# One FFN piece instead of two ahead of the transposes, in sixteen turns of a fused attention and FFN kernel

## The chip, the cores and the metric

The kernel runs on one core of one Trainium2 chip. A core has five engines that run beside each other, each through its own instructions in order: TensorE (PE: matmuls and transposes, results only to PSUM), VectorE (DVE), ScalarE (ACT), GpSimd (POOL) and SyncE (SP, which issues most transfers). PEld is TensorE's load of weights. The metric is the device time of one execution in microseconds.

## The reference, cut to what matters

Attention over 8 batches and 8 heads, 576 positions, 64 channels a head, that keeps only the 32 largest scores of each row, and a SwiGLU feed-forward network (FFN) behind it, all in float32:

```python
scores = scale * np.matmul(q, k.transpose(0, 1, 3, 2))          # (8, 8, 576, 576)
kth = np.partition(scores, -top_k, axis=-1)[..., -top_k:-top_k + 1]   # top_k = 32
scores = np.where(scores >= kth, scores, -1000000000.0)
attn = np.exp(scores - np.max(scores, axis=-1, keepdims=True))
attn = attn / (np.sum(attn, axis=-1, keepdims=True) + 1e-09)
attn_out = np.matmul(attn, v)
x = np.ascontiguousarray(attn_out.transpose(0, 2, 1, 3)).reshape(B * S, H * D)   # (4608, 512)
g = x @ w_gate                                                   # (512, 1536)
out = (g * (1.0 / (1.0 + np.exp(-g))) * (x @ w_val)) @ w_out     # (1536, 512)
```

## The kernel before, in words

**Units.** A unit is a batch, a tile of up to 128 query rows, and a pair of heads. A batch has five query tiles, four of 128 rows and one of 64, and four pairs of heads: 20 units, of which the first 16 are full and the last four short (their two heads share one tile of 128 partitions). There are 160 units, numbered from 0 here; 4 * NHP is 16, 9 * NHP is 36, and `units[n][1] < J` says that unit n is full.

**Turns.** The main loop runs one turn n per unit, and every turn works on several units at different stages. In program order a turn holds:
- in even turns, on TensorE, the scores of the next two units (L325, or L308 for short ones: `s`) and between them the product of the weights with v for two earlier units (L448: `av`). ScalarE scales the scores into `sc` (L330, L315) and copies `av` into the FFN's input `xT` (L465).
- `weigh(n - 1)` on ScalarE: a Prelu and an Exp that turn scores into unnormalised weights `e` (L374, L379), whose bias comes from GpSimd (L362).
- in slices, on VectorE, the search for the 32 largest of unit n: four rounds of MAX8 (L347) with a MATCH_REPLACE8 (L351) between. The first replacement of a unit writes its buffer of `e`, one of three.
- `pieces(2)`, then the pending ScalarE evictions, then `turn(n - 2)`: the transposes of the weights of unit n - 2 (L412: `etps`; nine of 128 x 128 for a full unit, five for a short one), which ScalarE copies to SBUF (L413: `et`). Then the pending GpSimd work and `pieces(1)`, `pieces(1)`.
- `normalize(n - 1)`: the reciprocal of the sums (L393, VectorE), and the multiplication of `e` by it: the first head on ScalarE (L397), the second on GpSimd (L399).
- `shift(n)` (L362), and `pieces(6)`.

In the first turns of a batch the q and k of later units are transposed as well (L271, L264: `kqps`, copied by L276, L267, L268).

**Pieces.** FFN work is cut into pieces and placed between the attention's steps. Two kinds matter. A projection piece is eight matmuls of `xT` with the gate or value weights (L517, in the first three blocks of 256 tokens; L604 later); two pieces fill one PSUM bank `f`, which ScalarE then evicts (`val` L544, or L537 to L539 for the gate) and GpSimd multiplies into `h` (L545, L540). A quarter piece is three matmuls of 128 x 256 of the output product (L670: `y_ps`, `x_ps`), which is done as seven products of halves with sums on GpSimd ahead of and behind them (L677, L685, L690, L718, L657) and evictions on ScalarE (L697, L704, L747, L759).

**Credit.** `pieces(k)` issues up to k pieces while the turn's credit is at least 1. A turn's credit is worked out beforehand (`share`); a projection piece costs 1, a quarter piece 0.75. The credit that the earlier calls leave is spent by the later ones, the last of which takes up to six pieces.

**Order.** After the loop every instruction of TensorE, VectorE, ScalarE and GpSimd is tied behind its predecessor on the same engine, so each engine runs exactly the order in which the program wrote them. Evictions and GpSimd products are kept in two lists (`on_act`, `on_pool`) and written when `flush` is called: at the start of a turn, behind the first `pieces`, behind the transposes (GpSimd's list), and in `piece` itself when more than one is pending, or when a new block begins.

**PSUM.** Of eight banks five go round among `s`, `av`, `etps` and `kqps` (pool `ps_t`) and three among `f`, `y_ps`, `x_ps` (pool `ps_f`). A tile can be written when the last reader of the tile five (three) allocations before it has finished.

Of the kernel before, what the change touches and what calls it, by code (L numbers as in the profile page):

```python
# [25 lines left out]
def kernel(  # L26
# [40 lines left out]
    J = S // P  # L67
    JP = J * P
    R = S - JP
    NHP = H // 2  # L70
# [134 lines left out]
    def rounding(n):  # L205
        for _ in range(n):
            next(weight, None)
# [73 lines left out]
    units = [(b, qt, hp) for b in range(B) for qt in range(J + 1) for hp in range(NHP)]  # L281
    state = {}

    def n_heads(qt):

        return 1 if qt == J else 2

    def scores(n):
        b, qt, hp = units[n]
        slab = preps[b * NHP + hp]  # L290
        sc = work.tile([P, 2 * S], FP32, tag="sc", name="sc", bufs=3)
        halves = [slice(0, D), slice(D, P)]
        half = S // 2

        def bank():
            return ps_t.tile([P, 512], FP32, tag="t", name="s")


        if qt == J:
            both = (slab, preps[b * NHP + hp + 1])  # L300
            banks = []
            for i in range(2):
                k0 = R + i * half
                two = [bank(), bank()]
                banks += [(i + 2 * u, ps) for u, ps in enumerate(two)]
                for u, (sl, ps) in enumerate(zip(both, two)):
                    for hh, d in enumerate(halves):
                        nc.tensor.matmul(  # L308
                            ps[halves[hh ^ u], 0:half],
                            sl[d, S + R : S + 2 * R],  # L310
                            sl[d, k0 : k0 + half],
                        )
            yield
            for i, ps in banks:
                nc.scalar.mul(sc[:, i * half : (i + 1) * half], ps[:, 0:half], scale)  # L315
            state[n + 1] = dict(sc=sc, at=S)
        else:
            q0 = S + 2 * R + qt * P
            banks = []
            for i in range(2):  # L320
                for hh, d in enumerate(halves):
                    ps = bank()
                    banks.append((i + 2 * hh, ps))
                    k0 = (1 - hh) * R + i * half
                    nc.tensor.matmul(  # L325
                        ps[:, 0:half], slab[d, q0 : q0 + P], slab[d, k0 : k0 + half]
                    )
            yield
            for i, ps in banks:
                nc.scalar.mul(sc[:, i * half : (i + 1) * half], ps[:, 0:half], scale)  # L330
        state[n] = dict(sc=sc, at=0)

    def select(n):

        nh = n_heads(units[n][1])
        sc = state[n]["sc"]
        m = small.tile([P, 2, TOP_K], FP32, tag="m", name="m")
        heads = [slice(t * S, (t + 1) * S) for t in range(nh)]
        at = state[n]["at"]
        from_ = [slice(at + t * S, at + (t + 1) * S) for t in range(nh)]  # L340
        e = work.tile([P, 2 * S], FP32, tag="e", name="e", bufs=3)
        state[n] |= dict(m=m, e=e, heads=heads, source=from_)
        cur = sc
        rounds = TOP_K // 8
        for r in range(rounds):
            for t, hs in enumerate(from_):
                nc.vector.max(m[:, t, 8 * r : 8 * r + 8], cur[:, hs])  # L347
                yield
            if r < rounds - 1:
                for t, hs in enumerate(heads):  # L350
                    nc.vector.match_replace(  # L351
                        e[:, hs], m[:, t, 8 * r : 8 * r + 8], cur[:, from_[t]], LOWEST
                    )
                    yield
                cur, from_ = e, heads
# [31 lines left out]
    def normalize(n):  # L387
        st = state[n]
        tot, e, heads = st.pop("tot"), st["e"], st.pop("heads")
        nh = len(heads)  # L390
        for t in range(nh if n >= AHEAD else 0):
            nc.vector.tensor_scalar_add(tot[:, t : t + 1], tot[:, t : t + 1], EPS)
        nc.vector.reciprocal(tot[:, 0:nh], tot[:, 0:nh])  # L393
        yield
        for t, hs in enumerate(heads):
            if t == 0 and n >= 3 * NHP:
                nc.scalar.mul(e[:, hs], e[:, hs], tot[:, t : t + 1])  # L397
            else:
                nc.gpsimd.tensor_tensor(  # L399
                    e[:, hs], e[:, hs], tot[:, t : t + 1].to_broadcast([P, S]), ALU.mult  # L400
                )
# [375 lines left out]
    def piece():  # L777

        if len(on_act) > 1:
            flush(on_act)  # L780
        if len(on_pool) > 1:
            flush(on_pool)
        for job in early_jobs[:]:
            cost = next(job, 0)
            if cost == 0:
                early_jobs.remove(job)
            elif cost is not None:
                return cost
        if early_jobs:
            return 0  # L790
        while True:
            if not current:
                if not todo or done.get(todo[0], 0) < tokens(todo[0], int(todo[0] >= HALVED)):
                    return 0
                flush(on_act)
                flush(on_pool)
                current.append(feed(todo.pop(0)))
            cost = next(current[0], 0)
            if cost == 0:
                current.pop()  # L800
                continue
            return cost or 0

    def fetch(n):

        b, qt, hp = units[n]
        i = b * NHP + hp
        if qt == 0:
            yield from prep(i)
        if qt == J and i + NHP < len(pairs):  # L810
            load(i + NHP)

    def share(n):


        others = 0.0
        for m, cost in [(m, 0.7) for m in valued(n)] + [(n - TURN, 0.6)]:
            if m >= 0:
                others += cost * (0.5 if units[m][1] == J else 1)
        others += 0.7 * len(scored(n))  # L820
        if units[n + 3][1] == 0:
            others += 0.6

        beside = 5.8 if n < AHEAD else 6.25
        least = 2.0 if n >= 3 * NHP and n % 2 == 0 else 0.0
        return max(least, beside * n_heads(units[n][1]) / 2 - others)

    def scored(n):

        ahead = [n + 1] if n < 2 else [] if n % 2 else [n + 1, n + 2]  # L830
        return [m for m in ahead if m < NU and (units[m][1] < J or m % 2 == 0)]
# [6 lines left out]
    def pieces(n):  # L838
        for _ in range(n):
            if credit[0] >= 1:  # L840
                credit[0] -= piece()
# [28 lines left out]
    for n in range(NU + 3):  # L870
        nh = n_heads(units[n][1]) if n < NU else 1
        topk = select(n) if n < NU else no
        norm = normalize(n - 1) if 0 <= n - 1 < NU else no
        nxt = [scores(m) for m in scored(n)]
        ahead = fetch(n + 3 if n else 2) if n + 3 < NU else no

        def dve(k, beside=True):

            for _ in range(k * nh):
                next(topk, None)  # L880
                due[0] += 5 / 6 if beside else 0
                if due[0] >= 1 and not (n == 0 and len(steps) == 5):
                    due[0] -= 1
                    steps.append(n)
                    rounding(1)

        if n >= NU - NHP:
            credit[0] = 8.0
        else:
            credit[0] = min(credit[0] + share(n), share(n) + 1)  # L890
        flush(on_act)
        flush(on_pool)
        if nxt and (n < 2 or len(nxt) > 1):
            run(nxt.pop(0))
        summed = finish_units(valued(n)) if valued(n) else no
        next(summed, None)
        if nxt:
            next(nxt[0])
        early[0]()
        if 0 <= n - 1 < NU:  # L900
            weigh(n - 1)
        run(summed)
        if nxt:
            run(nxt.pop())


        dve(2, beside=False)
        if n == 0:
            run(ahead)
            load(3)  # L910
            ahead = fetch(3)
        if n < NHP:
            load_v(n)
        pieces(2)
        flush(on_act)
        dve(1)
        dve(1)
        if 0 <= n - TURN < NU:
            run(turn(n - TURN))

        flush(on_pool)
        next(ahead, None)
        pieces(1)
        next(ahead, None)
        dve(1)
        pieces(1)
        if n < AHEAD:
            run(topk)
        run(norm)
        run(topk)  # L930
        if n < NU:
            shift(n)
        pieces(6)
# [50 lines left out]
```

## Time and profile before

| what | value |
|---|---|
| median of three runs | 1713.59 us (1713.14 to 1713.67) |
| the profiled execution: time, span | 1712.03 us, 1710.2 us |
| mean granted TensorE clock | 0.978 |
| turns 20 to 35 | about 223 to 386 us |
| nine transposes, start to start (251.33 to 252.31 us) | 0.98 us |
| two projection pieces, start to start (252.31 to 255.89 us) | 3.58 us |
| one quarter piece, start to start (272.46 to 273.76 us) | 1.30 us |

A row of the timeline gives start, duration, engine, source line, operation, output and inputs, shapes and count, and in brackets the idle time of the engine before it with the engine that ended it. A float32 matmul appears as two rows, so a projection piece is 16 rows and a quarter piece six; each transpose is one row. Matmuls overlap: the work that one costs is read from start to start, not from its duration. A table by stretch gives the busy time of each engine in a window, the granted clock and the transfers.

### The profile page before, as it was taken

How to read it: one execution, taken by the hardware profiler on the slowest of the kernel's cores; microseconds unless marked ns; L12 is line 12 of the kernel's file. 1: busy time of each engine (PE TensorE's matmuls, PEld its weight loads, DVE VectorE, ACT ScalarE, POOL GpSimd, SP SyncE). 2: the span in 40 equal slices, each digit the busy share in tenths (PEclk: the TensorE clock that was granted, in tenths of full speed). 3: DMA queues.
4: the chain of work that ended last, by engine and by line, in shares of the span. 5: the costliest groups of instructions: out<-in, count | busy, mean ns of one | idle time of the engine just before them, and what ended most of it. 6: DMA issues, size and time to landing. Idle time of an engine off the chain costs nothing.

```text
span 1710.2 us, 32128 instructions
## 1 busy us (share of the span) xinstructions
PE 1647.4 (96%) x11600; PEld 1398.2 (82%) x11600; DVE 1476.5 (86%) x3311; ACT 1259.5 (74%) x2901; POOL 799.0 (47%) x914
## 2 busy tenths in 40 slices
PE   5588999999999999999999999999999999999999
PEld 3477698987888887888888888888888888888887
DVE  7999899998989899997999989998999979999400
ACT  7899887877767787768676887777777778676531
POOL 4798545352444425353535334444344433535434
PEclk6699999999999999999999999999999999999999
DMA  7533120003000030001200030000400011000000
GB/s 210 139 112 99 29 72 2 14 1 79 22 13 1 15 86 14 1 8 42 51 14 1 13 74 27 2 13 2 98 1 13 2 44 29 13 2 13 1 13 13
DMA packets 109310, 59.74 MB, mean 35 GB/s; under 512 B 88544, under 2 KB 96992, under 8 KB 109152
## 3 DMA queue, kind: packets, MB, share of 16 engines
q1 hardware_dynamic: 108016, 57.37, 12.9%
q8 instruction: 91, 1.49, 0.4%
q14 instruction: 67, 0.55, 0.1%
q10 hardware_dynamic: 1136, 0.33, 0.1%
HBM read 48.23 MB, written 9.44 MB: 34 GB/s over the span
## 4 chain that ended last, share of the span: by engine, by line
PE 88%; DVE 5%; ACT 4%; DMA 1%; POOL 1%; issue 1%; SPq 0%; POOLq 0%; ACTq 0%
PE f L604 37%; PE x_ps L670 10%; PE av L448 9%; PE s L325 8%; PE y_ps L670 8%; PE etps L412 7%; PE f L517 6%; DVE m L347 2%; DVE e L351 2%; PE kqps L271 1%; PE o_ps L569 1%; PE s L308 1%; ACT e L379 1%; DVE size L124 1%; ACT e L374 0%
## 5 line engine op out<-in xcount | busy, mean ns | idle before, releaser
L347 DVE MAX8 m<-e 128x8 f32<-128x576 f32 x864 | 617.9, 755 | 3.3
L351 DVE MATCH_REPLACE8 e<-m,e 128x576 f32<-128x576 f32 x576 | 425.4, 748 | 0.0
L604 PE MATMUL f<-xT,wg 128*128 128x256 f32 x1440 | 335.9, 382 | 1.3 <-ACT xT L465 1.3
L604 PE MATMUL f<-xT,wv 128*128 128x256 f32 x1440 | 331.4, 380 | 0.0
L604 PEld LDWEIGHTS f<-xT,wg 128*128 128x128 f32 x1440 | 268.9, 190 | 49.0 <-issue 13.1
L604 PEld LDWEIGHTS f<-xT,wv 128*128 128x128 f32 x1440 | 268.2, 190 | 37.5 <-issue 3.8
L640 POOL TENSOR_TENSOR h<-h,half_g 128x512 f32<-128x512 f32 x90 | 114.7, 1275 | 349.2 <-ACT h L639 349.2
L330 ACT ACTIVATE sc<-s 128x288 f32<-128x288 f32 x512 | 170.4, 431 | 105.2 <-PE s L325 104.6
L413 ACT COPY et<-etps 128x512 f32<-128x512 f32 (+1 forms) x448 | 183.6, 486 | 66.0 <-PE etps L412 65.6
L379 ACT ACTIVATE e<-e,bias 128x576 f32<-128x576 f32 x288 | 221.7, 780 | 12.7 <-POOL bias L362 9.7
L374 ACT ACTIVATE e<-sc,m 128x576 f32<-128x576 f32 x288 | 212.3, 792 | 0.6 <-DVE m L347 0.5
L351 DVE MATCH_REPLACE8 e<-m,sc 128x576 f32<-128x576 f32 x288 | 212.6, 748 | 0.0
L412 PE MATMUL etps<-ident,e 128*128 128x128 f32 x1312 | 178.2, 280 | 33.7 <-POOL e L399 15.0
L347 DVE MAX8 m<-sc 128x8 f32<-128x576 f32 x288 | 204.0, 747 | 7.5 <-ACT sc L330 7.5
L412 PEld LDWEIGHTS etps<-ident,e 128*128 128x128 f32 x1312 | 156.2, 144 | 54.7 <-POOL e L399 19.2
L645 POOL TENSOR_TENSOR h<-h,val 128x512 f32<-128x512 f32 x90 | 114.8, 1275 | 155.0 <-ACT val L644 152.4
L325 PE MATMUL s<-kqT 64*128 64x288 f32 x1024 | 169.2, 441 | 13.7 <-ACT sc L330 7.5
L399 POOL TENSOR_TENSOR e<-e,tot 128x576 f32<-128x576 f32 x140 | 161.1, 1154 | 28.5 <-DVE tot L393 28.2
L448 PE MATMUL av<-et,v 128*64 128x128 f32 (+1 forms) x2560 | 158.0, 268 | 0.0
L448 PEld LDWEIGHTS av<-et,v 128*64 128x64 f32 x2560 | 137.7, 140 | 5.9 <-ACT kqT L268 2.7
L325 PEld LDWEIGHTS s<-kqT 64*128 64x128 f32 x1024 | 94.2, 190 | 58.3 <-issue 18.4
L397 ACT ACTIVATE e<-e,tot 128x576 f32<-128x576 f32 x148 | 119.1, 805 | 21.7 <-DVE tot L393 21.6
(86 smaller groups left out, 2249.1 us busy)
## 6 DMA issues: line engine op xcount, KB each, us to landing
v<-in_v_dram SPq DMA_DIRECT2D x32, 256.0 KB, 3.3
kq_in<-in_k_dram SPq DMA_DIRECT2D x63, 128.0 KB, 2.8
kq_in<-in_q_dram SPq DMA_DIRECT2D x63, 128.0 KB, 2.9
w<-in_moe_w_gate_dram SPq DMA_DIRECT2D x12, 512.0 KB, 3.8
w<-in_moe_w_val_dram SPq DMA_DIRECT2D x12, 512.0 KB, 3.8
w<-in_moe_w_out_dram SPq DMA_DIRECT2D x12, 512.0 KB, 3.5
out_dram<-o SPq DMA_DIRECT2D x38, 128.0 KB, 2.4
out_dram<-o SPq DMA_DIRECT2D x16, 256.0 KB, 2.5
```

Of the source, the lines that this page charges most:

```text
L325: nc.tensor.matmul(ps[:, 0:half], slab[d, q0 : q0 + P], slab[d, k0 : k0 + half])
L330: nc.scalar.mul(sc[:, i * half : (i + 1) * half], ps[:, 0:half], scale)
L347: nc.vector.max(m[:, t, 8 * r : 8 * r + 8], cur[:, hs])
L351: nc.vector.match_replace(e[:, hs], m[:, t, 8 * r : 8 * r + 8], cur[:, from_[t]], LOWEST)
L374: nc.scalar.activation(e[:, hs], sc[:, at], AF.Prelu, bias=m[:, t, TOP_K - 1 : TOP_K], scale=-1.0, alpha=SMALL,)
L379: nc.scalar.activation(e[:, hs], e[:, hs], AF.Exp, bias=bias[:, t : t + 1], scale=-1.0 / SMALL, accum_out=tot[:, t : t + 1],)
L399: nc.gpsimd.tensor_tensor(e[:, hs], e[:, hs], tot[:, t : t + 1].to_broadcast([P, S]), ALU.mult)
L412: nc.tensor.transpose(ps[:, c * P : (c + 1) * P], e[:, k0 : k0 + P], ident[:])
L413: nc.scalar.copy(et[:, c0 : c0 + cn, :], ps[:, 0 : cn * P].rearrange("p (c j) -> p c j", c=cn),)
L448: nc.tensor.matmul(av[d, i, 0:ql], weights_, moving, start=c == (0 if last else J), stop=c == (J if last else J - 1),)
L604: nc.tensor.matmul(ps[:, i, :], w[:, kc, m * P : (m + 1) * P], x[:, kc, :], start=(kc == 0), stop=(kc == KC - 1),)
L670: nc.tensor.matmul(ps, lhsT, T[i][m], start=m == 0, stop=m == MQ - 1)
```

## The change

In the turns 16 <= n < 36 whose unit is full, which are the sixteen turns 20 to 35, one piece instead of two is asked for in front of the transposes, and two instead of one right behind them. All other turns are unchanged, and no work is added or left out.

```diff
@@ -911,7 +911,8 @@
             ahead = fetch(3)
         if n < NHP:
             load_v(n)
-        pieces(2)
+        soon = 4 * NHP <= n < 9 * NHP and units[n][1] < J
+        pieces(1 if soon else 2)
         flush(on_act)
         dve(1)
         dve(1)
@@ -920,7 +921,7 @@
 
         flush(on_pool)
         next(ahead, None)
-        pieces(1)
+        pieces(2 if soon else 1)
         next(ahead, None)
         dve(1)
         pieces(1)
```

## The prediction

> **What bounds the kernel now.** I read the busy times first, then the same by stretch for the 16 turns that the change touches (223 to 386 us), then TensorE's waits there, then the timeline and the chain of work inside single turns. "Before" and "after" are the two kernels; turn n is the loop's n-th pass and transposes the weights e of unit n-2.
>
> From the page's first part and the table by stretch (width, then busy time and instruction count of PE, PEld, DVE, ACT, POOL, then PE clock and DMA):
>
> ```profile
> PE 1647.4 (96%) x11600; PEld 1398.2 (82%) x11600; DVE 1476.5 (86%) x3311; ACT 1259.5 (74%) x2901; POOL 799.0 (47%) x914
> ...
> 244.00:266.00 22.00, 22.00 (x221) 20.89 (x220) 21.28 (x48) 18.11 (x42) 8.21 (x10) 1.00 0.11 28
> 266.00:285.00 19.00, 19.00 (x138) 16.11 (x138) 16.18 (x35) 13.85 (x33) 11.32 (x16) 1.00 0.00 1
> 285.00:306.00 21.00, 20.65 (x163) 18.03 (x164) 21.00 (x46) 15.64 (x37) 10.22 (x14) 1.00 0.07 26
> 306.00:327.00 21.00, 21.00 (x204) 19.79 (x202) 19.73 (x43) 17.02 (x40) 7.53 (x9) 1.00 0.01 2
> 386.00:402.00 16.00, 13.82 (x146) 10.99 (x146) 13.85 (x31) 12.86 (x32) 6.13 (x10) 1.00 0.30 69
> ```
>
> TensorE is busy for the whole of three of these stretches and lacks 0.35 us in the third; only at 386 to 402, behind the changed turns, does it lack 2.2 us. VectorE has idle time in the same stretches (2.8 of 19 us at 266). So TensorE sets the pace. Its own waits in the region (223 to 400 us; total, times, longest) are few:
>
> ```profile
> PE etps L412 <- ACT e L397: 1.7, 1, 1.7
> PE s L325 <- ACT et L413: 0.6, 1, 0.6
> PE etps L412 <- ACT xT L465: 0.4, 1, 0.4
> PE etps L412 <- POOL e L399: 0.3, 1, 0.3
> ```
>
> The 1.7 and the 0.4 are at 392 to 396 us and the 0.6 at 223, outside the changed turns. Inside them TensorE waits once, 0.35 us for GpSimd. A change of order that leaves TensorE's work the same can therefore gain little here, and every new wait of TensorE goes to the end: its queue is full again from 400 us on, but for single stalls such as one of 2.3 us at 660 to 680.
>
> Two turns show how near the wait is. Turns 24 and 25, from the timeline (start, duration, instruction, count):
>
> ```profile
> 272.46 1.46 PE L670 MATMUL y_ps<-wo,h 128*128 128x256 f32 x6
> 273.39 1.27 POOL L545 TENSOR_TENSOR h<-h,val 128x512 f32<-128x512 f32 x1 [6.22 <-ACT val L544]
> 273.76 1.15 PE L412 MATMUL etps<-ident,e 128*128 128x128 f32 x9
> 274.62 2.10 POOL L677 TENSOR_TENSOR xT<-h 128x256 f32<-128x256 f32 x3
> 274.74 1.46 PE L670 MATMUL y_ps<-wo,h 128*128 128x256 f32 x6
> 276.04 1.46 PE L670 MATMUL x_ps<-t,xT 128*128 128x256 f32 x6
> 276.68 1.14 POOL L399 TENSOR_TENSOR e<-e,tot 128x576 f32<-128x576 f32 x1
> 277.33 1.31 PE L412 MATMUL etps<-ident,e 128*128 128x128 f32 x9
> ```
>
> The transposes at 277.33 need the second head of e from GpSimd, ready at 276.68+1.14 = 277.82: they are just held. Turn 26 to 27 is the same, in the chain of work (start, length):
>
> ```profile
> 291.69 0.49 ACT p L704
> ...
> 293.77 1.24 POOL p L657
> 295.01 2.07 POOL h L718 x3
> 297.08 1.11 POOL e L399
> 298.19 0.04 issue
> 298.24 0.76 PE etps L412 x5
> ```
>
> **The change part by part.** In 16 turns (20 to 35) the second piece in front of the transposes goes behind them. The program's order shows no instruction added or removed and the same pieces in every turn; only the place of nine (in two turns five) transposes against one piece moves. The piece is a projection in turns 20 to 23 and 28 to 33: 32 rows of L517 take 252.31 to 255.89, 3.58 us, so 1.79 a piece. It is a quarter piece of the output product in turns 24 to 27, 34, 35: 272.46 to 273.76, 1.30 us. On ScalarE four val evictions (L544, 0.58 us) go behind the et copies and the L397 multiply, and on GpSimd four h products (L545, 1.28) fall behind L399 and the L362 behind it. SyncE and the loads keep their order. Those engines move no work into TensorE's path except through the three waits below.
>
> *Gain.* TensorE starts its transposes earlier but has as much to do: 0, bounded by the one wait inside (0.5 us start to start at 297.6). VectorE gains: it waited 6.0 us in the region for transposes to free e, and TensorE does not wait for VectorE; what hides the gain is TensorE's full queue. If that cover were gone, 6.0 would be the bound.
>
> *Turn 22, a wait for a PSUM bank.* The five banks of ps_t go round, so the transposes of an even turn reuse first the bank of av, then two of the scores. In turn 22 one projection piece behind 247.66 ends at 247.66+0.09+1.79 = 249.54 (0.09: 251.33-247.66 less two pieces). ScalarE copies av out (L465) from 249.88 to 250.13 and the scores from 250.03 (four of 0.43 in 1.31, so the second ends 250.75). TensorE starts 0.05 after such a copy (392.71 to 392.76), so at 250.18 not 249.54: 0.64, and 0.07 more for the third bank: **0.71 us**. ScalarE cannot be sooner: it works without a break from 244.11. Bounds: 0, if another bank comes first, to 1.85 (all four score copies, 251.34, awaited). I take 0.71 because the wait at 392.76 names L465. The margins to L465 elsewhere: turn 20 229.33 against 228.38; 24 272.45 against 271.32; 26 290.99 against 290.47; 28 312.15 against 311.07; 30 333.28 against 332.20; 32 352.62 against 352.30; 34 about 374.7 against 373.99. No wait.
>
> *Turns 24 and 25, a wait for GpSimd.* L545, L677 and L399 keep their order there, and start from the end of the wv piece at 272.45, which does not move; so e is ready at 277.82 as before. TensorE's order becomes: transposes 272.45 to 273.43, two y pieces to 276.02, then the next transposes, held after four of nine (276.46) until 277.88. Their end stays where it was, at 278.48, but one x piece that stood in front is still to do: **1.30 us** lost. Behind the held transposes stand all further pieces.
>
> *Turns 26 and 27, the same.* L704, the L657 sums, L718 and L399 keep their order and time (298.19). TensorE reaches the transposes at 295.9 (289.72+1.30+0.98+1.30+2.59), is held after four (296.3) until 298.24, and again has one more piece to do: **1.30 us**. Bounds of each of these two: 0, if GpSimd's chain comes 1.3 earlier, to 1.74, if the first head (L397, ScalarE) came late too and all nine transposes stood behind the wait instead of five (four more of 0.11, as nine take 0.98). I take the piece: e's time is fixed in both orders, and what stood in front of the wait is what is lost.
>
> *The other turns.* In odd turns 23, 29, 31, 33, 35 the slack of the transposes to e was 3.5, 3.8, 2.0, 3.5 and 3.6 us, and the copies and L397 in front of e move up with the even turn's transposes: 0. In turn 21 the transposes come at 236.21 against L397's end at 236.06: 0, by 0.1. In turn 36 nothing is moved, and the stall of 1.75 there hangs on ScalarE's L759, which starts at 388.95 behind the last x piece of TensorE: it shifts along, it absorbs nothing.
>
> Sum: 0.71+1.30+1.30 = **3.31 us**. The profiled execution has a span of 1710.2 and a time of 1712.03 us, 1.56 below the median of the runs, 1713.59. It becomes 1715.34, and the median **1716.9**, 0.19% more. What a measurement can tell from no change is about 0.2%, 3.43 us, so the forecast lies at that line.
>
> [...] In 223 to 402 us TensorE's rows follow each other with no idle but the named, while its weight loads are busy 158.0 of 179 us. [...]
>
> **The rivals.**
> 1. *More bank waits.* The evictions put off leave ScalarE later by one of them, 0.58 us, when the scores come. Then turn 22 costs 0.58 more and turn 32, whose margin is 0.32, 0.26: sum 4.15, time 1717.7. For it: ScalarE runs without a break in both turns. Against: the evictions fall into its idle time (it waits 8.9 us for scores in the region). It decides from 0.12 us of lateness on, where the sum passes 3.43.
> 2. *Swallowed at the boundary (not slower).* If the 1.75 us stall before 395.77 hung on VectorE, which comes sooner by the change, it would take up 1.75 of the 3.31: 1.56, time 1715.2. For it: reciprocals of e gate L397 too. Against: L759 and the L374 behind it wait for TensorE.
> 3. *VectorE sets the pace (faster).* If the transposes that free e paced the turns, the 6.0 us of VectorE's waits came back, less 3.31: 1710.9. Against: TensorE at 100% in the stretches above. It decides when TensorE has idle time of its own there, over 3.31 us.
> 4. *GpSimd is sooner.* If h products put off free it in turns 24 and 26, both 1.30 vanish: 0.71, time 1714.3. Against: those two turns keep GpSimd's order.
>
> **How the numbers follow.** Forecast case 0.60, rival 1 0.25, rival 2 0.06, rival 4 0.04, rival 3 0.05. The forecast case spreads by half a microsecond to both sides of the line at 3.43: 0.33 within, 0.27 slower. Slower 0.27+0.25 = 0.52; same 0.33+0.06+0.04 = 0.43; faster 0.05. Range: below, rival 4 (1714.3) is taken in down to 1714.2 and rival 3 left out; above, three waits at their upper bounds would give 1.85+1.74+1.74 = 5.33, 1718.9. The forecast's own range is 1716.4 to 1717.4.
>
> **What would show it.** Right: in after, GpSimd's L399 still ends near 277.8 and 298.2 plus what was lost before, with TensorE's L412 held there some 1.4 and 1.9 us; a new wait of L412 for L465 near 250; the gap before 395.77 still about 1.75. VectorE's waits for L412 shrink from 6.0. Wrong: L399 early in turns 24 or 26, TensorE waits in more turns than 22, 25 and 27, or a changed gap at the boundary.

## The result and the profile after

The change makes the kernel 0.2% slower: 1716.74 us in the median of 14 runs (1714.92 to 1718.14) against 1713.29 of 14 runs before (1711.75 to 1714.59), a ratio of 1.002 with a 95% interval of 1.0013 to 1.0027. That is 3.45 us, with an interval from 2.2 to 4.6. The forecast was 1716.9.

Two spans of single profiles are a poor measure here: 1715.3 against 1710.2, 5.1 us apart. When the first scores of turn 20 start, at 223.13 us before and 225.00 after, the two already differ by 1.87 us, though up to there no instruction differs. So the runs are compared below on the **stretch** from the first scores row of turn 20 to that of turn 38: 177.33 us before, 180.44 after, +3.11. Behind it both need the same time again, 1309.78 and 1309.88 us.

The busy times of after, from the first part of the page:

```profile
PE 1651.0 (96%) x11600; PEld 1402.0 (82%) x11600; DVE 1478.5 (86%) x3311; ACT 1259.9 (73%) x2901; POOL 799.9 (47%) x914
```

And the table by stretch of after (width, then busy time and count of PE, PEld, DVE, ACT, POOL, then PE clock and DMA; the windows are those shown of before, moved to where the same turns lie now):

```profile
246.00:268.50 22.50, 22.02 (x218) 20.67 (x218) 22.50 (x50) 18.24 (x42) 8.55 (x9) 1.00 0.10 28
268.50:289.00 20.50, 19.24 (x139) 16.27 (x138) 17.38 (x39) 13.88 (x33) 12.04 (x16) 1.00 0.01 2
289.00:311.00 22.00, 20.34 (x161) 17.82 (x162) 21.53 (x47) 15.55 (x37) 9.40 (x13) 1.00 0.07 25
391.00:407.00 16.00, 13.85 (x147) 11.01 (x146) 14.14 (x31) 12.89 (x32) 5.16 (x8) 1.00 0.30 70
```

TensorE, full in the first two of these before, now lacks 0.48, 1.26 and 1.66 us in the first three. Its waits in 223 to 405 us (total, times, longest) name the engines:

```profile
PE etps L412 <- POOL e L399: 2.9, 2, 1.7
PE etps L412 <- ACT e L397: 1.7, 1, 1.7
PE etps L412 <- ACT xT L465: 0.9, 2, 0.5
PE s L325 <- ACT et L413: 0.6, 1, 0.6
```

The 0.3 us for GpSimd has become 2.9, and a second wait for L465 has come; the other two are those of before. From one first scores row to the next (two turns), after less before:

| turns | 20, 21 | 22, 23 | 24, 25 | 26, 27 | 28 to 33 | 34, 35 | 36, 37 |
|---|---|---|---|---|---|---|---|
| us | 0.00 | +0.77 | +1.32 | +1.31 | 0.00 each | -0.29 | +0.01 |

The whole loss lies in three pairs of turns. Turns 24 and 25 in TensorE's timeline of after (start, duration, instruction, count, idle time before it):

```profile
275.10 1.15 PE L412 MATMUL etps<-ident,e 128*128 128x128 f32 x9
276.08 2.75 PE L670 MATMUL y_ps<-wo,h 128*128 128x256 f32 x12
278.68 0.60 PE L412 MATMUL etps<-ident,e 128*128 128x128 f32 x4
280.54 0.77 PE L412 MATMUL etps<-ident,e 128*128 128x128 f32 x5 [1.26 <-POOL e L399]
281.14 2.76 PE L670 MATMUL x_ps<-t,xT 128*128 128x256 f32 x12
```

And in GpSimd's timeline of after:

```profile
276.03 1.28 POOL L545 TENSOR_TENSOR h<-h,val 128x512 f32<-128x512 f32 x1 [6.22 <-ACT val L544]
277.27 2.11 POOL L677 TENSOR_TENSOR xT<-h 128x256 f32<-128x256 f32 x3
279.34 1.14 POOL L399 TENSOR_TENSOR e<-e,tot 128x576 f32<-128x576 f32 x1
```

GpSimd's three steps stand where they stood, 2.64 to 2.66 us later (1.87 from the start and 0.77 from turn 22). Four transposes of the first head run, five wait for the second head; then both x pieces are still to do, where before one was done. Turn 27 is the same (TensorE's and GpSimd's timelines of after; before, the wait there was 0.35 us):

```profile
299.95 0.60 PE L412 MATMUL etps<-ident,e 128*128 128x128 f32 x4
302.21 0.77 PE L412 MATMUL etps<-ident,e 128*128 128x128 f32 x5 [1.66 <-POOL e L399]
301.00 1.16 POOL L399 TENSOR_TENSOR e<-e,tot 128x576 f32<-128x576 f32 x1
```

In turn 22 the copy of av is done ahead of the transposes before (ScalarE's and TensorE's timelines):

```profile
249.88 0.25 ACT L465 COPY xT<-av 128x128 f32<-128x128 f32 x1
251.33 1.15 PE L412 MATMUL etps<-ident,e 128*128 128x128 f32 x9
```

In after it holds them:

```profile
251.76 0.25 ACT L465 COPY xT<-av 128x128 f32<-128x128 f32 x1
252.06 1.27 PE L412 MATMUL etps<-ident,e 128*128 128x128 f32 x9 [0.48 <-ACT xT L465]
```

### The profile page after: what moved, and what is told of

Read it like the earlier page. It is cut to its first block, busy times and chain, and to the rows that moved or that the text cites. A ratio compares the mean times of both kernels' runs of the same rounds, so it can differ in the third digit from the quotient of the medians.

```text
span 1715.3 us, 32129 instructions
## 1 busy us (share of the span) xinstructions
PE 1651.0 (96%) x11600; PEld 1402.0 (82%) x11600; DVE 1478.5 (86%) x3311; ACT 1259.9 (73%) x2901; POOL 799.9 (47%) x914
## 4 chain that ended last, share of the span: by engine, by line
PE 87%; DVE 6%; ACT 5%; POOL 1%; DMA 1%; issue 1%; SPq 0%; POOLq 0%; ACTq 0%
PE f L604 36%; PE x_ps L670 10%; PE av L448 9%; PE s L325 8%; PE y_ps L670 7%; PE etps L412 7%; PE f L517 5%; DVE m L347 3%; DVE e L351 2%; PE kqps L271 1%; PE o_ps L569 1%; ACT e L379 1%; PE s L308 1%; DVE size L124 1%; ACT e L374 1%
## 5 line engine op out<-in xcount | busy, mean ns | idle before, releaser
L412 PE MATMUL etps<-ident,e 128*128 128x128 f32 x1312 | 178.1, 280 | 35.6 <-POOL e L399 17.8
L412 PEld LDWEIGHTS etps<-ident,e 128*128 128x128 f32 x1312 | 156.0, 144 | 56.7 <-POOL e L399 21.9
L399 POOL TENSOR_TENSOR e<-e,tot 128x576 f32<-128x576 f32 x140 | 161.2, 1155 | 34.9 <-DVE tot L393 34.5
L397 ACT ACTIVATE e<-e,tot 128x576 f32<-128x576 f32 x148 | 119.3, 806 | 19.5 <-DVE tot L393 19.4
```

What stands on the lines that cost most here:

```text
L399: nc.gpsimd.tensor_tensor(e[:, hs], e[:, hs], tot[:, t : t + 1].to_broadcast([P, S]), ALU.mult)
L412: nc.tensor.transpose(ps[:, c * P : (c + 1) * P], e[:, k0 : k0 + P], ident[:])
```

## The experiments

In each table row below, "stretch" lies between the same two rows of scores as above; steps are against the kernel before.

| run | stretch, us | turns 22, 23 | 24, 25 | 26, 27 | 34, 35 | 36, 37 |
|---|---|---|---|---|---|---|
| before | 177.33 | | | | | |
| before again | 177.37 | 0.00 | +0.02 | 0.00 | +0.01 | +0.01 |
| the change | 180.44 | +0.77 | +1.32 | +1.31 | -0.29 | +0.01 |
| the change again, twice | 180.42, 180.41 | +0.77, +0.76 | +1.31 | +1.30, +1.31 | -0.30 | 0.00 |
| turns 22, 25, 27 alone | 180.70 | +0.76 | +1.31 | +1.29 | +0.01 | 0.00 |
| the other thirteen turns | 177.04 | 0.00 | +0.01 | 0.00 | -0.30 | 0.00 |
| second heads on ScalarE | 177.07 | +0.76 | -0.16 | -0.57 | -0.30 | 0.00 |
| ScalarE sooner in turn 22 | 181.04 | 0.00 | +1.31 | +1.29 | -0.30 | +1.40 |
| no piece ahead in 25 and 27 | 187.45 | +0.76 | +4.13 | +5.51 | -0.30 | 0.00 |
| three pieces ahead in 25 and 27 | 177.64 | 0.00 | -0.16 | -0.57 | -0.30 | +1.33 |
| a version meant to beat both | 174.24 | 0.00 | -0.16 | -0.57 | -4.18 | +1.82 |

### Is the stretch a measure? The kernel before again

No edit.

> The kernel before, once more, for the measure itself. The two profiles differed by 1.87 us already at 223 us, where no instruction differs. My theory: that is the start (loads, TensorE's clock below full), which differs from one execution to the next by some 1 to 2 us, while the stretch from turn 20 to turn 38 is repeated within 0.05 us: 177.33. Rival: the stretch itself varies by 1 us or more, and the readings of the other runs mean little.

Measured: 177.37, with turn 20 at 225.59 us instead of 223.13. The stretch is repeated to 0.04 us, the start is not, by 2.46. Of these 2.46 us some 1.6 come between the scores rows at 153 and at 178 us, where the clock was granted at 0.5 from 168.67 to 172.08 us, in this profile of the two alone. Readings of a tenth of a microsecond in the stretch hold where no such fall of the clock lies in it.

### Three turns alone

```diff
-        soon = 4 * NHP <= n < 9 * NHP and units[n][1] < J
+        soon = n in (22, 25, 27)
```

> The piece is moved in turns 22, 25 and 27 alone; the other thirteen turns are as before. Measured on the stretch from the first scores of turn 20 to the first scores of turn 38 (177.33 us before, 180.44 us with all sixteen moved, so +3.11). My theory, three waits of TensorE in just these turns: +0.77 + 1.32 + 1.30 = +3.4 (the 0.3 that turns 34 and 35 gave back is not to be had here). Rival, a small cost in each of the sixteen turns (evictions put off): 3/16 of 3.1, +0.6. Rival, the even turns of the two pairs (24 and 26) are what costs: +0.8.

Measured: 180.70, +3.37. The three turns carry all of the loss. Since of the two pairs only the odd turn is moved here, it is the piece that no longer stands ahead of the odd turn's transposes that costs, not that of turns 24 and 26.

### The other thirteen

```diff
-        soon = 4 * NHP <= n < 9 * NHP and units[n][1] < J
+        soon = 4 * NHP <= n < 9 * NHP and units[n][1] < J and n not in (22, 25, 27)
```

> The other way round: the piece is moved in thirteen turns and not in turns 22, 25 and 27. My theory: the stretch becomes as long as before or shorter by the 0.3 us of turns 34 and 35: 177.0 to 177.3; whole time the same as before within what can be measured. Rival, a small cost in each turn: +2.5, 179.8. Rival, late evictions (all four moved val evictions but one are still moved here): +1 or more.

Measured: 177.04, and 1712.86 us in the median of 11 runs, a ratio of 0.9998 (0.9989 to 1.0007) to before. A small cost in every turn is out, and so are the evictions that are put off: three of the four (all but turn 22's) still are here.

### The second heads on ScalarE

The change, with in `normalize`:

```diff
-            if t == 0 and n >= 3 * NHP:
+            if (t == 0 or n in (23, 25)) and n >= 3 * NHP:
```

> All sixteen turns moved as in the change, but in units 23 and 25 the second head of the weights is multiplied on ScalarE too, not on GpSimd behind its sums: 0.8 us more on ScalarE, 1.15 less on GpSimd. My theory: TensorE's waits for GpSimd in turns 25 and 27 (1.26 and 1.66 us of idle time in the profile after) are gone, and only the 0.77 of turn 22 less the 0.3 of turns 34 and 35 stay: stretch about 177.8. The transposes may still wait some 0.1 to 0.4 us for the second multiply on ScalarE. Rival, the order of the pieces itself or the evictions cost the time: 180.4 as after.

Measured: 177.07; 1713.06 us in the median, a ratio of 1.0 (0.9991 to 1.0009). TensorE's order is that of the change, and both losses are gone; so are 0.16 and 0.57 that the kernel before still lost at the same places. That is more than expected: no wait for the second multiply was left. Turns 24 and 25 in TensorE's timeline of this run:

```profile
275.29 2.76 PE L670 MATMUL y_ps<-wo,h 128*128 128x256 f32 x12
277.89 1.15 PE L412 MATMUL etps<-ident,e 128*128 128x128 f32 x9
```

ScalarE's timeline of this run has the two heads ready at 276.10+1.47 = 277.57, ahead of the transposes at 277.89:

```profile
276.10 1.47 ACT L397 ACTIVATE e<-e,tot 128x576 f32<-128x576 f32 x2
```

So it was L399's place in GpSimd's line (behind L545 and L677 in turn 25, behind the sums L657 and L718 in turn 27) that made the order of the pieces costly; with the heads off that line the same order costs nothing there.

### No piece ahead in turns 25 and 27

The change, and `held = n in (25, 27)`:

```diff
-        pieces(1 if soon else 2)
+        pieces(0 if held else 1 if soon else 2)
...
-        pieces(2 if soon else 1)
+        pieces(3 if held else 2 if soon else 1)
```

> As the change, but in turns 25 and 27 no piece at all stands ahead of the transposes, and three behind. My theory, the time at which GpSimd hands over the weights is fixed and whatever no longer stands in front of the wait is lost: 1.30 us more in each, stretch 183.0; the idle time of TensorE in front of the held transposes grows from 1.3 and 1.7 to about 2.6 and 3.0 us. Rival, GpSimd's sums follow TensorE's order and come sooner too: 180.4 as after, waits as after.

Measured: 187.45, 4.45 us more than expected. GpSimd's time did not move: L399 of turn 25 starts 54.31 us behind the first scores of turn 20, in the change 54.34. The waits for it came near what was expected (2.12 and 2.94 us, the first with 0.21 for L397 ahead of it), but behind them TensorE ran slower. TensorE's timeline of this run:

```profile
278.67 1.33 PE L412 MATMUL etps<-ident,e 128*128 128x128 f32 x5 [2.12 <-POOL e L399]
279.79 2.47 PE L670 MATMUL y_ps<-wo,h 128*128 128x256 f32 x6
```

From the start of the five transposes to the next piece it took 0.60 us in the change (280.54 to 281.14) and 1.12 here (278.67 to 279.79). The table by stretch of this run, whose last but two column is the granted clock:

```profile
278.00:282.00 4.00, 3.33 (x11) 2.93 (x12) 4.00 (x10) 2.96 (x8) 2.82 (x5) 0.57 0.00 0
```

The clock was granted at 0.5 from 278.42 to 281.83 (3.41 us) and from 302.31 to 309.14 (6.83 us). In the first TensorE worked 3.16 us of 3.41, in the second 5.99: at half the clock that costs half of it, by estimate, 1.6 and 3.0. With 1.30 for the piece each, 2.9 and 4.3 over the change; measured 2.81 and 4.20. So a piece more costs what was expected, 1.30 us, and the rest goes with the clock, an effect of its own.

### ScalarE sooner in turn 22

The change, with at the start of a turn:

```diff
-        flush(on_act)
+        if n != 22:
+            flush(on_act)
         flush(on_pool)
```

> As the change, but in turn 22 the pending evictions of a gate and a value product (L544, L537 to L539, 2.3 us on ScalarE) are written behind the copies of the scores instead of in front of them. My theory of turn 22: the transposes wait for a PSUM bank because ScalarE, late by these evictions, copies av out late; with them out of the way the copy ends about 0.7 to 0.8 us sooner and the wait of 0.5 us idle (0.77 start to start) is gone: stretch 180.44 - 0.77 = 179.7. Rival, the cost of turn 22 lies elsewhere (the second piece of the product, its entry): 180.4.

Measured: the step of turns 22 and 23 is 0.00 instead of 0.77. TensorE's timeline of this run has no idle time ahead of the transposes:

```profile
249.00 1.15 PE L412 MATMUL etps<-ident,e 128*128 128x128 f32 x9
```

In ScalarE's timeline of this run the copy of av ends 5.32 us behind the turn's first scores (243.45), where it was 6.14 in the change (252.01 behind 245.87):

```profile
248.52 0.25 ACT L465 COPY xT<-av 128x128 f32<-128x128 f32 x1
```

The stretch as a whole is 181.04 and not 179.7, because behind the old wait of 1.75 us in turn 37, where the edit changes nothing, the clock was granted at 0.5 from 397.52 to 400.94: +1.40.

### Three pieces ahead in turns 25 and 27

The thirteen, and in the two turns the opposite of the change (`held = n in (25, 27)`):

```diff
-        pieces(1 if soon else 2)
+        pieces(3 if held else 1 if soon else 2)
...
-        pieces(2 if soon else 1)
+        pieces(0 if held else 2 if soon else 1)
```

> Moved in the thirteen turns that cost nothing; turn 22 as before; in turns 25 and 27 three pieces ahead of the transposes and none right behind, the other way from the change. My theory: the waits for GpSimd that the kernel before still had there (0.11 and 0.51 us) go too, and the 0.3 us of turns 34 and 35 come back: stretch 177.33 - 0.9 = 176.4, shorter than in both kernels; in the whole time no more than -0.05%, which cannot be told from no change. Rival, the waits of before were TensorE's own change of work, not GpSimd: 177.0.

Measured: -0.16, -0.57 and -0.30, close to what was expected; the stretch is 177.64 all the same, for at the boundary (turns 36 and 37) the clock was granted at 0.5 again, from 396.29 to 399.70 us (+1.33). 1712.92 us in the median against 1714.17 of the runs beside it, a ratio of 0.9994 (0.9985 to 1.0003).

### The change again, twice

No edit.

> The change once more, for the scatter. In three of the seven runs so far TensorE's granted clock fell to 0.5 for 3.41 us or a multiple right behind a wait of 1.7 us or more, and the stretch then grew by another 1.3 to 4.2 us; in the same wait of other executions it did not. Theory: the clock is decided in steps of 3.41 us, and falls when most of a step was idle; where a step begins differs from execution to execution. Then the stretch is 180.4 where no wait fills a step, and about 181.8 where the wait at the boundary (2.1 us of idle time in 3.8) does. Rival: these steps down belong to the kernels they were seen in, and the change always takes 180.4.

> The same once more: 180.4, or about 181.8 with a clock step at the boundary; the waits of turns 22, 25 and 27 by themselves as in the first profile (0.77, 1.32, 1.31 us).

Measured: 180.42 and 180.41, each step within 0.02 us of the first profile, and no clock step in the stretch in either.

### A version meant to beat both

The thirteen and the two second heads on ScalarE, and three quarter pieces of turn 35 kept for turn 36: one ahead of its transposes, two between these and those of turn 37.

```diff
+        soon = (4 * NHP <= n < 9 * NHP and units[n][1] < J and n not in (22, 25, 27)) or n == 36
...
-        pieces(1)
+        pieces(0 if n == 35 else 1)
         if n < AHEAD:
...
-        pieces(6)
+        pieces(0 if n == 35 else 6)
```

> A version meant to beat both: the piece is moved in the thirteen turns that cost nothing, the second heads of units 23 and 25 are multiplied on ScalarE, and three quarter pieces of turn 35 are kept for turn 36, one ahead of its transposes and two between them and those of turn 37, where TensorE stood idle (0.38 and 1.75 us). Expected from the steps measured so far: -0.16 and -0.57 (turns 25, 27), -0.3 (turn 34), -2.13 (the two waits at the boundary): stretch 177.33 - 3.2 = 174.2, whole time some 3 us or 0.18% under the kernel before, and a little more in the median if the waits at the boundary cost a clock step in some executions. Rival: the boundary is paced by ScalarE and VectorE, and TensorE only waits elsewhere: 176.3.

Measured: stretch 174.24, and 1709.12 us in the median of 11 runs against 1713.0 of the runs of before beside them: a ratio of 0.9979 (0.997 to 0.9988): 0.2% faster than the kernel before, clear of the scatter. The change was not run beside it; its own median is 1716.74. (The steps -4.18 and +1.82 are the work moved from one pair of turns to the next; their sum is -2.36.) The table by stretch has TensorE busy there, where before it worked 13.82 of 16 us:

```profile
386.00:402.00 16.00, 15.74 (x156) 12.74 (x155) 15.22 (x38) 13.35 (x32) 7.38 (x11) 1.00 0.11 26
```

## Why the prediction was right

- **What bounds.** TensorE without idle time in the region: right. The stretch lost what TensorE waited, and nothing was made up later (1309.78 and 1309.88 us). The weight loads left 12% free in 223 to 402 us (158.0 of 179 us busy), yet no part of the loss came back: whether a new wait can be made up in a stream of fixed order was told by the rows without gaps. A small misreading: the 2.3 us at 660 to 680 us are two stalls, of 0.99 and 1.32 us.
- **Turn 22**, 0.71 forecast: 0.77 measured, and 0.00 with ScalarE out of the way.
- **Turns 24 and 25, 26 and 27**, 1.30 each: 1.32 and 1.31. That exactly one piece is lost, whatever the length of the wait, was the step that mattered: TensorE's end is set by GpSimd in both orders. Shown by the second heads on ScalarE, which take both losses away, and by L399, which starts at the same time in the stretch with one piece fewer ahead. The holds of some 1.4 and 1.9 us that were to be seen are 1.42 and 1.82 start to start (1.26 and 1.66 idle).
- **The other turns**, 0: right but for turns 34 and 35, which gave 0.29 back. The forecast bounded the gain of earlier transposes by TensorE's one named wait and overlooked a smaller one: before, TensorE started the last x pieces at 386.06, late for L718 by 0.19 start to start, and these pieces took 0.1 longer than in after (2.79 and 2.69 us). With turn 34's transposes sooner, ScalarE ends its weights, the eviction L704 and GpSimd's sums sooner. The thirteen turns show the gain alone (-0.30); its path through ScalarE is read from the rows and was not tried by itself.
- **The boundary.** That the stall before 395.77 shifts along: right, 1.75 us in both. Before, ScalarE has no idle time from L759 (388.95) to the end of the L397 that ends the stall (395.72), so it does not hang on VectorE; and pieces put into it take it away.
- **The sum.** 3.31 forecast; 0.77+1.32+1.31-0.29 = 3.11 in the stretch, 3.45 between the medians. The medians cannot tell 3.31 from 3.11 (2.2 to 4.6); that they lie within 0.2 us of the forecast is in part luck, and the steps in the stretch are the evidence.
- **The clock.** The sum has no term for the clock. That was right for this change, but hung on a size that the forecast did not work out: the idle time in one step of 3.41 us. In the twelve profiles, from 140 to 1630 us, the granted clock fell behind six steps, with 1.96 to 2.11 us of it each (last section); a step with a new wait in it had at most 1.42 us. The new waits of 0.48, 1.26 and 1.66 us were followed by no fall of the clock in three profiles; the longer ones of the run with no piece ahead were. There the two waits are 0.9 and 1.3 us longer (2.12 and 2.94), the clock was granted at 0.5 for 3.41 and 6.83 us, and the stretch loses 10.12 us instead of 3.11.
- **Rivals.** More bank waits: none in turn 32. Swallowed at the boundary: no. VectorE as the pace: its waits for L412 fell from 6.0 to 3.8 us, but those for ScalarE's L384 rose from 0.8 to 6.2, so VectorE did not gain as the forecast had it, and the stretch grew by what TensorE waited. GpSimd sooner in turns 24 and 26: no.

## What to carry to other kernels

Where an engine is full and runs a fixed order, moving work costs what it uncovers: for each moved step, compare the time at which its input is handed over by the other engine with the time at which the step now arrives. If the input's time does not move and the step was held already, the loss is the work that no longer stands in front of it, not the length of the wait (turns 25 and 27: one piece, 1.30 us). If the step had slack, the loss is that work less the slack (turn 22: a piece of 1.79 us, of which 0.77 was lost). And the same wait can be put to use: keep pieces back for the places where TensorE is known to stand idle.

## What the runs showed of the hardware

In the traces of the kernel before and of the change every interval at one granted clock, the last apart, lasted 3.41 us or a whole multiple of it: the kernel before has intervals of 3.41, 6.83, 10.24, 13.65, 20.48 and 30.72 us up to 138 us, then one of 1505.28 at 1.00. For all twelve profiles, from 140 to 1630 us, TensorE's idle time between its matmul rows was summed in each such step of 3.41 us. After every step with 1.76 us of idle time or less the next was granted at 1.00 (if the step itself was); after each of the six with 1.96 to 2.11 us the next was granted at 0.5. No step there had between 1.76 and 1.96 us. One of the six falls lasted two steps, in the run with no piece ahead: there the first slow step had 0.84 us of idle time itself; the slow steps with 0.25 us or less were followed by 1.00.

So two waits that make some 2.1 us together were followed in some profiles by a fall of the clock, which cost 1.3 to 1.6 us, and in others by none. The old waits at 165 to 168 us (1.61 and 0.45 us in the kernel before) and at 392 to 396 us (0.38 and 1.75) were followed by a step at 0.5 in two profiles each, of the twelve and the eleven that have them; at 165 to 168 us one of the two was the kernel before again, from 168.67 us on. In the first profile of the kernel before steps end at 165.77 and at 394.47 us, inside these waits: the idle time is parted into 0.73 and 1.33 us there and 0.82 and 1.33 us here, and the clock stayed at 1.00. The falls are part of why profiles of one kernel differ by some us. The time at which turn 20 starts differed by up to 3.8 us (222.58 to 226.35), of which some 1.6 are such a step: without the two profiles that have it at 168 us the range is 222.58 to 225.00.
